# Loading the first Q and K heads as f32 over the hardware queues and casting them on chip, in a fused attention and SwiGLU kernel

## The chip, the cores and the metric

The kernel runs on one core of one Trainium2 chip. The core has a matrix engine (PE, TensorE), a vector engine (DVE), an activation engine (ACT), GpSimd (POOL) and a sync engine (SP). Matrix products read SBUF and write PSUM, which has 8 banks; DVE and ACT read PSUM and write SBUF. DMA transfers between memory and SBUF are issued from POOL (the software queue) or from SP and ACT (the hardware queues), and 16 DMA engines carry them. The metric is the device time of one execution in microseconds (us), as a median of several.

## The reference, cut to what matters

```python
batch, n_heads, seq, head_dim = (8, 12, 448, 64)
scores = scale * np.matmul(q, k.transpose(0, 1, 3, 2))
attn = np.maximum(scores, 0.0) ** 2 / S
x = np.matmul(attn, v)                     # then heads side by side: x is 3584 x 768
rms = np.sqrt(np.mean(x * x, axis=-1, keepdims=True) + 1e-06)
xn = x / rms * rms_g
g = xn @ w_gate                            # 768 x 1536
silu = g * (1.0 / (1.0 + np.exp(-g)))
out = (silu * (xn @ w_val)) @ w_out        # 1536 x 768
```

All inputs and the output are float32. The attention has no softmax: scores go through a relu and a square, so nothing has to be known of a whole row before it is used. The kernel computes in bf16 with f32 accumulation.

## The kernel before, in words

The kernel goes through the 8 batches in order. For each batch it computes the attention of 12 heads, taken as 6 pairs of heads (a pair fills 128 partitions, 64 rows for each head), then a norm over the 768 columns, then the two-layer feed-forward part. The attention of batch b+1 or b+2 is computed while the feed-forward of batch b runs: the weight products come as a "stream" of small steps, and attention work is put between them.

Before the first stream step there is nothing to put the attention between. This stretch is called the head here. In it batch 0 alone is worked on, in two halves of 224 query rows. For a pair of heads the steps are:

- load Q and K: the DMA converts f32 to bf16 on the way. K of batch 0 lands in `wo_sb`, the buffer that later holds the output weights; Q lands in its own tile. (`load`, L278; one load is 2 or 4 heads for batch 0.)
- transposes on PE into a PSUM bank (`transposes`, L412; 14 small products for K at L421 and 8 for Q at L429), then one copy by DVE to `qkT` (L439).
- scores on PE into a pair of PSUM banks (L503, and L521 for the last 64 rows of keys, called the rest), one block of 896 or 448 columns at a time. There are three such pairs of banks in the head.
- relu of the block by ACT (L469) or DVE (L467), then its square by DVE (L472).
- products with V (L607), evicted by ACT (L642), squared by DVE (L646), summed over columns by PE (L904).

When three such sums are in, ACT takes the logarithm and the exponential that make the root of the norm (L712, L716), DVE scales (L721), and the stream of weight products (L856) begins.

The order of instructions on every engine is written out when the kernel is built, by a planner. It keeps a clock for each engine, a cost for each step, and an estimate of when each DMA lands (`arrives` and `pool_dma`: a start after 2.7 us and a rate for each kind of load). It always takes the step that can begin first, and among those that are ready the one of best rank; transposes go before scores. Its times decide only the order; at run time each instruction waits for its own data, but an engine never runs an instruction ahead of one that stands before it.

Where the planner sees PE idle for 0.3 us or more, `fill` (L1118) puts products of ones with zeros there (L1129), as many as fit at 0.1 us each. Their result is not used.

POOL issues all loads on one software queue. A load waits until the eighth load before it has landed. The order for batch 0 is: Q and K of heads 0 and 1, of heads 2 and 3, then the identity matrix for the transposes (made on POOL), Q and K of heads 4 to 7, of heads 8 to 11, then V, then the weights in four slices. SP loads the norm's weights `g_sb` (L380) first; ACT loads a function table first (L392).

Of the kernel before, what the change touches and what calls it, by code (L numbers as in the profile page):

```python
# [8 lines left out]
FP32 = mybir.dt.float32  # L9
BF16 = mybir.dt.bfloat16  # L10
ALU = mybir.AluOpType
ACT = mybir.ActivationFunctionType

NCH = 4
U = 7
# [51 lines left out]
class Planner:  # L67
# [28 lines left out]
    def start(self, op, e, t):  # L96
        for x in op.on:
            self.lists[x].remove(op)
        dur = op.on[e]() if callable(op.on[e]) else op.on[e]
        if e == "PE":  # L100
            dur += self.changed(op.form() if callable(op.form) else op.form)
        self.free[e] = t + dur
        op.engine, op.begun, op.left = e, t, t + dur
        op.done = op.ends(t) if op.ends else t + dur + {"ACT": 0.17, "DVE": 0.13, "PE": 0.22}.get(e, 0.1)
        op.fn(op)
# [67 lines left out]
def kernel(  # L173
# [11 lines left out]
    nc = tc.nc  # L185
    P = nc.NUM_PARTITIONS
    B, H, S, D = q.shape
    T, DM = out.shape
    _, F = moe_w_gate.shape
    assert (T, DM) == (B * S, H * D) and 2 * D == P and S % NCH == 0 and B % 2 == 0 and S == U * D  # L190
    PC = S // NCH
# [34 lines left out]
    def tiles(n, shape, dtype, name):  # L226
        return [work.tile(shape, dtype, name=f"{name}{i}", tag=f"{name}{i}") for i in range(n)]
# [14 lines left out]
    hT = tiles(1, [P, FT, 2 * S], BF16, "hT")[0]  # L242

    plan = Planner(8)
    plan.singles = single
    add = plan.add


    ld, qkT, landed, behind_of = {}, {}, {}, {}
    src_of = {"q": q, "k": k, "v": v}  # L250
    PE_T = 2
    dma_free = [2.2]

    def arrives(kb, rate):
        def ends(t):
            dma_free[0] = max(dma_free[0], t + 2.7) + kb / rate
            return dma_free[0] + 0.2
        return ends

    def pool_dma(cost, kb, rate, start, deps=()):  # L260

        deps = list(deps) + queue[-8:-7]
        queue.append(add(Op({"POOL": cost}, lambda op: start(), deps, ends=arrives(kb, rate))))
        return queue[-1]
# [3 lines left out]
    def stage(nm, b):  # L268
        runs = nm == "v" or b < PE_T
        n, w = (PC, NCH) if nm == "q" else (P, UH)  # L270
        if (nm, b) not in ld:
            shape = [n, H, w * D] if runs else [n, w, H * D]
            ld[nm, b] = ldpool.tile(shape, BF16, name=nm + "b", tag=nm + "b")
            if nm == "k" and runs:
                nc.vector.memset(ld[nm, b][D:, :, (UH - 1) * D :], 0.0)
        return ld[nm, b]

    def load(nm, b, h0=0, h1=H, deps=()):  # L278
        runs = nm == "v" or b < PE_T
        src = src_of[nm][b, h0:h1]  # L280
        if (nm, b) == ("k", 0):

            def runs_of_seven():
                nc.gpsimd.dma_start(
                    out=wo_sb[:D, h0:h1, :S], in_=src.rearrange("h (p u) d -> p h (u d)", p=D)
                )

            ops = [pool_dma(0.7, D * U * D * 4 * (h1 - h0) / 1e3, 300.0, runs_of_seven, deps)]
            landed.setdefault((nm, b), {}).update({h: ops for h in range(h0, h1)})
            return  # L290
        if nm == "q":
            parts = [(slice(0, PC), PC, 0, NCH)]
        else:
            parts = [(slice(0, D), D, 0, UH), (slice(D, P), D, UH if nm == "k" else UH - 1, U)]
        ops = []
        for prt, n, u0, u1 in parts:
            kb = n * (u1 - u0) * D * 4 * (h1 - h0) / 1e3

            def whole(prt=prt, n=n, u0=u0, u1=u1):
                dma = nc.gpsimd.dma_start(  # L300
                    out=stage(nm, b)[prt, h0:h1, : (u1 - u0) * D],
                    in_=src.rearrange("h (p u) d -> p h (u d)", p=n)[:, :, u0 * D : u1 * D],
                )
                if b >= PE_T and not u0:
                    tc.add_manual_dep(dma.ins, turned[b][-1].ins.name, behind)

            if runs:
                ops.append(pool_dma(0.72, kb, (300.0 if nm == 'q' else 345.0) if b == 0 else 400.0, whole, deps))
                continue
            step = u1 - u0 if nm == "q" else 1  # L310
            for u in range(u0, u1, step):

                def piece(prt=prt, n=n, u=u, u0=u0, step=step):
                    to = stage(nm, b)[prt].rearrange("p u (h d) -> p u h d", d=D)
                    rows = src.rearrange("h (p u) d -> p u h d", p=n)
                    behind_of[b] = nc.gpsimd.dma_start(  # L316
                        out=to[:, u - u0 : u - u0 + step, h0:h1, :], in_=rows[:, u : u + step]
                    )

                ops.append(  # L320
                    pool_dma(2.3 if step > 1 else 0.75, kb * step / (u1 - u0), 280.0, piece, deps)
                )
        landed.setdefault((nm, b), {}).update({h: ops for h in range(h0, h1)})

    def new_qkT(b):
        qkT[b] = qtpool.tile([P, HP, 2, S], BF16, name="qkT", tag="qkT")

    turned, made = {}, {}

    def transpose_dma(b, deps):  # L330
        jobs = [("k", c) for c in range(UH)] + [("q", c) for c in range(NCH)]
        turned[b] = []
        for nm, c in jobs:

            def turn(op, nm=nm, c=c):
                if b not in qkT:
                    new_qkT(b)
                n = (P if c < UH - 1 else D) if nm == "k" else PC
                at = c * P if nm == "k" else c * PC
                op.ins = nc.sync.dma_start_transpose(  # L340
                    out=qkT[b][:, :, 0 if nm == "k" else 1, at : at + n], in_=ld[nm, b][:n, c, :]
                ).ins
                if (nm, c) == ("k", 0):
                    tc.add_manual_dep(op.ins, behind_of[b].ins.name, behind)

            need = list(deps) + landed["q", b][0] + landed["k", b][0]
            turned[b].append(add(Op({"SP": 0.1}, turn, need, ends=arrives(170, 120.0))))
# [3 lines left out]
    wo_sb = wpool.tile([P, FT, DM], BF16, name="wo_sb", tag="wo")  # L351
# [21 lines left out]
    busy_bf = const.tile([P, S], BF16, name="busy_bf", tag="busy_bf")  # L373
    nc.vector.memset(busy_bf[:], 0.0)
    ident = const.tile([P, P], BF16, name="ident", tag="ident")
    eps_col = const.tile([P, 1], FP32, name="eps_col", tag="eps_col")
    nc.vector.memset(eps_col[:], eps)
    scrap = const.tile([P, 1], FP32, name="scrap", tag="scrap")
    g_sb = wpool.tile([P, KT], FP32, name="g_sb", tag="rmsg")
    nc.sync.dma_start(out=g_sb[:], in_=moe_rms_g.rearrange("(kt p) -> p kt", p=P))  # L380

    LN_EXP, SILU = 6, 18
    held = [None]
# [4 lines left out]
    def act_set(n):  # L388
        if held[0] != n:
            held[0] = n  # L390
            name = nc.get_next_instruction_name()
            nc.scalar.add_instruction(  # L392
                mybir.InstLoadActFuncSet(name=name, act_func_set_id=n, ins=[], outs=[])
            )

    act_set(LN_EXP)
    plan.free.update({"POOL": 1.3, "PE": 1.3, "DVE": 2.0, "ACT": 2.3, "SP": 1.2})

    behind = mybir.DependencyInfo(mybir.DependencyClass.Sync, mybir.DependencyReason.DATA)

# [342 lines left out]
    class Stream:  # L743
# [8 lines left out]
        def add(self, groups):  # L752
            self.todo += groups
# [364 lines left out]
    def fill(t0, t1):  # L1118
        if not fill_on[0] or t1 - t0 < 0.3:
            return  # L1120
        s = None
        for x in single[::-1]:
            if plan.banks_free(x.banks) <= t0:
                s = x
                break
        if s is None:
            return
        for _ in range(int((t1 - t0 - 0.15) / 0.1)):
            nc.tensor.matmul(out=s.tile[:, :HS], lhsT=ones_bf[:], rhs=busy_bf[:, :HS], start=True, stop=True)  # L1129

    plan.fill = fill

    load("q", 0, 0, 2)
    load("k", 0, 0, 2)
    load("q", 0, 2, 4)
    load("k", 0, 2, 4)
    made["ident"] = add(Op({"POOL": 0.6}, lambda op: masks.make_identity(nc, ident[:])))
    for h in (4, 8):
        load("q", 0, h, h + 4)
        load("k", 0, h, h + 4)  # L1140
    load("v", 0, 0, 6)
    load("v", 0, 6, 12)
    for s in range(NSL):
# [79 lines left out]
```

## Time and profile before

| | us |
|---|---|
| median of 3 runs | 444.3 (443.7 to 445.11) |
| the profiled execution | 441.81 |
| its span, first to last instruction | 440.0 |
| PE busy in the span | 433.7 |
| DVE, ACT, POOL busy in the span | 242.8, 264.5, 77.8 |
| first fill product on PE | 1.30 |
| first transposes on PE | 7.07 |
| first eviction on ACT | 8.92 |
| root of the norm on ACT | 25.59 |
| first weight product on PE | 27.26 |

All times in the trace count from the start of the span. The page shows how long each engine is busy and which groups of instructions cost most; the chain of work follows back from the last instruction, at each step, to what released it. Rows in order of time have the start, the time, the engine, the line, what it writes and reads, and in brackets how long the engine was idle before and what ended that. An engine that is 55% busy over the whole span can still be the one that everything waits for in one stretch of it, so windows of the span are read beside the averages.

### The profile page before, as it was taken

The numbers are of one execution on the slowest core, as the hardware profiler recorded it, in microseconds if no ns is written. First come the engines' busy times: TensorE is split into PE (matmuls) and PEld (weight loads), VectorE is DVE, ScalarE is ACT, GpSimd is POOL, SyncE is SP. The second block draws the span as 40 slices with busy tenths as digits, with TensorE's granted clock in tenths as the row PEclk, the third lists the DMA queues.
The fourth block names the chain that finished last, engine by engine and source line by source line (L and its number), as shares of the span: only waits on it lengthen the run. The fifth ranks groups of instructions, "written<-read, shape, count | busy, mean of one in ns | idle before, by whom it ended". The sixth has DMA issues, their size and how long they took to land.

```text
span 440.0 us, 17134 instructions
## 1 busy us (share of the span) xinstructions
PE 433.7 (99%) x7861; PEld 355.3 (81%) x7861; DVE 242.8 (55%) x414; ACT 264.5 (60%) x389; POOL 77.8 (18%) x98
## 2 busy tenths in 40 slices
PE   8999999999999999999999999999999999999996
PEld 6678877677978997787778997689988998688875
DVE  2977588466746564575655456466755356432210
ACT  3983497677648675675758666576657656342222
POOL 7622620060052053043000340010000000000000
PEclk9999999999999999999999999999999999999999
DMA  8999999799889789799906899781001300020013
GB/s 106 197 204 201 201 192 103 139 175 96 109 89 195 87 143 175 85 146 174 40 4 100 154 183 52 113 145 39 3 4 36 105 9 4 1 85 27 3 37 109
DMA packets 130392, 44.75 MB, mean 102 GB/s; under 512 B 102289, under 2 KB 126865, under 8 KB 130321
## 3 DMA queue, kind: packets, MB, share of 16 engines
q0 software_dynamic: 90944, 24.39, 62.1%
q1 hardware_dynamic: 38992, 18.94, 22.1%
q8 instruction: 61, 1.00, 1.0%
q10 hardware_dynamic: 384, 0.34, 0.3%
q14 instruction: 11, 0.08, 0.1%
HBM read 48.76 MB, written 11.01 MB: 136 GB/s over the span
## 4 chain that ended last, share of the span: by engine, by line
PE 94%; DMA 3%; ACT 2%; issue 0%; DVE 0%; POOL 0%; POOLq 0%
PE psP L856 76%; PE psS L607 7%; PE psS L485 5%; DMA vb<-in_v_dram 3%; PE psP L1129 2%; PE psP L429 1%; PE psS L521 1%; PE psS L503 1%; ACT r L469 1%; ACT acc L469 1%; PE psP L421 0%; ACT x L469 0%; PE psP L904 0%; ACT xT L642 0%; DVE acc L472 0%
## 5 line engine op out<-in xcount | busy, mean ns | idle before, releaser
L856 PE MATMUL psP<-xn,wg_sb 64*64 64x448 bf16 (+1 forms) x2304 | 234.0, 338 | 0.0
L856 PE MATMUL psP<-xn,wv_sb 64*64 64x448 bf16 (+1 forms) x2304 | 216.9, 338 | 1.0 <-issue 1.0
L469 ACT ACTIVATE r<-psS 128x896 bf16<-128x896 f32 (+1 forms) x164 | 145.4, 919 | 61.1 <-PE psS L485 32.9
L856 PEld LDWEIGHTS <-wg_sb 64*64 64x64 bf16 (+1 forms) x2304 | 134.2, 105 | 18.3 <-issue 3.8
L856 PEld LDWEIGHTS <-wv_sb 64*64 64x64 bf16 (+1 forms) x2304 | 134.3, 105 | 14.8 <-issue 3.4
L856 PE MATMUL psP<-wo_sb,hT 64*128 64x384 bf16 (+2 forms) x1563 | 139.8, 321 | 0.0
L472 DVE TENSOR_TENSOR r<-r 128x896 bf16<-128x896 bf16 (+1 forms) x165 | 98.7, 616 | 68.6 <-ACT r L469 67.6
L856 PEld LDWEIGHTS <-hT 64*128 64x128 bf16 (+1 forms) x1563 | 99.8, 97 | 23.9 <-issue 3.5
L941 DVE TENSOR_TENSOR hT<-sil,psP 128x448 bf16<-128x448 bf16 (+1 forms) x108 | 61.0, 566 | 56.7 <-PE psP L856 37.6
L927 ACT ACTIVATE sil<-psP 128x448 bf16<-128x448 f32 (+1 forms) x108 | 54.7, 507 | 57.7 <-PE psP L856 53.9
L1001 ACT COPY ost<-psP 128x384 f32<-128x384 f32 (+1 forms) x52 | 24.5, 471 | 41.0 <-PE psP L856 40.5
L485 PE MATMUL psS<-qkT 64*64 64x448 bf16 (+1 forms) x412 | 48.4, 350 | 0.0
L607 PE MATMUL psS<-r,vb 64*64 64x448 bf16 (+1 forms) x716 | 44.6, 335 | 0.4 <-DMA vb<-in_v_dram 0.2
L300 POOL DMA_DIRECT2D vb<-in_v_dram x20 | 14.3, 725 | 171.5 <-PE psP L856 97.0
L721 DVE SCALAR_TENSOR_TENSOR xn<-xT,g_sb,rstd 128x448 bf16<-128x448 bf16 (+1 forms) x54 | 30.2, 628 | 25.9 <-ACT rstd L716 25.9
L316 POOL DMA_DIRECT2D kb<-in_k_dram x42 | 33.4, 1022 | 19.3 <-DMA vb<-in_v_dram 11.3
L607 PEld LDWEIGHTS <-vb 64*64 64x64 bf16 x756 | 26.6, 106 | 8.6 <-issue 1.6
L642 ACT ACTIVATE xT<-psS 128x896 bf16<-128x896 f32 (+1 forms) x27 | 22.7, 841 | 10.5 <-PE psS L607 10.5
L485 PEld LDWEIGHTS <-qkT 64*64 64x64 bf16 (+1 forms) x412 | 21.7, 103 | 4.1 <-issue 1.1
L392 ACT ACT_TABLE_LOAD x16 | 20.5, 1283 | 1.0 <-PEq L1207 0.7
L652 DVE TENSOR_TENSOR x<-xT 128x896 f32<-128x896 bf16 x14 | 15.2, 1086 | 3.5 <-ACT xT L642 3.5
L654 DVE TENSOR_TENSOR acc<-acc,x 128x896 f32<-128x896 f32 x14 | 15.3, 1092 | 0.5
(58 smaller groups left out, 151.8 us busy)
## 6 DMA issues: line engine op xcount, KB each, us to landing
vb<-in_v_dram POOLq DMA_DIRECT2D x12, 384.0 KB, 8.1
qb<-in_q_dram POOLq DMA_DIRECT2D x6, 672.0 KB, 15.1
kb<-in_k_dram POOLq DMA_DIRECT2D x42, 96.0 KB, 12.4
out_dram<-ost SPq DMA_DIRECT2D x7, 336.0 KB, 3.0
wg_sb<-in_moe_w_gate_dram POOLq DMA_DIRECT2D x4, 576.0 KB, 15.5
wv_sb<-in_moe_w_val_dram POOLq DMA_DIRECT2D x4, 576.0 KB, 17.2
wo_sb<-in_moe_w_out_dram POOLq DMA_DIRECT2D x2, 1152.0 KB, 15.1
out_dram<-ost SPq DMA_DIRECT2D x8, 288.0 KB, 3.0
```

Source lines behind the costliest of these rows:

```text
L316: behind_of[b] = nc.gpsimd.dma_start(out=to[:, u - u0 : u - u0 + step, h0:h1, :], in_=rows[:, u : u + step])
L392: nc.scalar.add_instruction(mybir.InstLoadActFuncSet(name=name, act_func_set_id=n, ins=[], outs=[]))
L469: nc.scalar.activation(out=op.view, in_=src, func=ACT.Relu)
L472: nc.vector.tensor_tensor(out=rl.view, in0=rl.view, in1=rl.view, op=ALU.mult)
L485: nc.tensor.matmul(out=ps[m0:m1, hh, :S], lhsT=qkT[b][prt, j, 0, c * P + m0 : c * P + m1], rhs=qkT[b][prt, j, 1, :], start=True, stop=True,)
L607: mm = nc.tensor.matmul(out=ps[hh * D : (hh + 1) * D, jj, :w], lhsT=vb[prt, 2 * (j + jj) + hh, u * D : (u + 1) * D], rhs=r[prt, hh, :], st ...
L642: nc.scalar.mul(out=xTs[b][:, j : j + 2, lo : lo + w], in_=me.ps.tile[:, :, :w], mul=inv_attn)
L721: nc.vector.scalar_tensor_tensor(out=xns[b][:, kt, lo : lo + w], in0=xTs[b][:, kt, lo : lo + w], scalar=g_sb[:, kt : kt + 1], in1=rstd[:, ...
L856: mm = nc.tensor.matmul(out=self.ps[m0:m1, : self.w], lhsT=self.lhsT(i)[prt, m0:m1], rhs=self.rhs(i)[prt], start=(half == 0 and i == 0), s ...
L927: nc.scalar.activation(out=s[:, :w], in_=g.ps[:, :w], func=ACT.Silu)
L941: nc.vector.tensor_tensor(out=hT[:, fb, o : o + w], in0=sil[b, fb, lo][1][:, :w], in1=g.ps[:, :w], op=ALU.mult,)
L1001: nc.scalar.copy(out=to, in_=g.ps[:, :w])
```

## The change

Heads 0 to 3 of batch 0's Q and K are no longer loaded by POOL with conversion. A new function, `load_exact`, loads them as f32 into `hT` (the buffer for hidden values, not used until the feed-forward part, seen as f32): K from SP's queue, Q from ACT's, two heads in each load. Then DVE or ACT, whichever the planner finds free first, casts them to bf16 into the places where the transposes read them: one step for each head of K, one for two heads of Q. As planned, ACT takes both steps of Q and one of two steps of K in each half, and DVE takes the other step of K.

The loads of heads 4 to 7 become POOL's first, and the identity is made behind them; its zeros are set by DVE. `g_sb` goes behind K on SP, and ACT's table load behind its two issues. The planner's numbers change too: the rate for the loads of batch 0, when the engines are first free, and 0.19 us for a fill product before 5.5 us. As a result 17 fill products stand ahead of the first transposes instead of 42, and the order of the head changes: the transposes of the third and fourth pair come after three score blocks instead of six.

```diff
+    def load_exact(h0, h1):
+        plain = hT.bitcast(FP32)
+        for nm, eng, n, r in (("k", "SP", D, U), ("q", "ACT", PC, NCH)):
+            w = r * D
+            at = slice(h0 + (4 if nm == "q" else 0), h1 + (4 if nm == "q" else 0))
+            def start(op, nm=nm, eng=eng, n=n, at=at, w=w):
+                (nc.sync if eng == "SP" else nc.scalar).dma_start(
+                    out=plain[:n, at, :w],
+                    in_=src_of[nm][0, h0:h1].rearrange("h (p u) d -> p h (u d)", p=n),
+                )
+            moved = add(Op({eng: 0.47}, start, ends=arrives(S * D * 4 * (h1 - h0) / 1e3, 380.0, 1.9), rank=-9))
+            step = 1 if nm == "k" else 2
+            for h in range(h0, h1, step):
+                def cast(op, nm=nm, n=n, h=h, w=w, step=step):
+                    to = wo_sb[:D, h : h + step, :S] if nm == "k" else stage("q", 0)[:, h : h + step, :]
+                    src = plain[:n, h + (4 if nm == "q" else 0) : h + step + (4 if nm == "q" else 0), :w]
+                    if op.engine == "DVE":
+                        nc.vector.tensor_copy(out=to, in_=src)
+                    else:
+                        nc.scalar.copy(out=to, in_=src)
+                c = add(Op({"DVE": 0.07 + step * w * 1.042e-3, "ACT": 0.05 + step * w * 0.833e-3}, cast, [moved], rank=-5))
...
-            ops = [pool_dma(0.7, D * U * D * 4 * (h1 - h0) / 1e3, 300.0, runs_of_seven, deps)]
+            ops = [pool_dma(0.7, D * U * D * 4 * (h1 - h0) / 1e3, 370.0, runs_of_seven, deps)]
...
-                ops.append(pool_dma(0.72, kb, (300.0 if nm == 'q' else 345.0) if b == 0 else 400.0, whole, deps))
+                ops.append(pool_dma(0.72, kb, 370.0 if b == 0 else 400.0, whole, deps))
...
+    nc.vector.memset(ident[:], 0.0)
...
-    nc.sync.dma_start(out=g_sb[:], in_=moe_rms_g.rearrange("(kt p) -> p kt", p=P))
...
-    act_set(LN_EXP)
-    plan.free.update({"POOL": 1.3, "PE": 1.3, "DVE": 2.0, "ACT": 2.3, "SP": 1.2})
+    plan.free.update({"POOL": 1.3, "PE": 1.3, "DVE": 1.4, "ACT": 0.75, "SP": 0.75})
...
-        for _ in range(int((t1 - t0 - 0.15) / 0.1)):
+        while t0 + (0.19 if t0 < 5.5 else 0.1) <= t1 - 0.15:
+            t0 += 0.19 if t0 < 5.5 else 0.1
             nc.tensor.matmul(out=s.tile[:, :HS], lhsT=ones_bf[:], rhs=busy_bf[:, :HS], start=True, stop=True)
...
-    load("q", 0, 0, 2)
-    load("k", 0, 0, 2)
-    load("q", 0, 2, 4)
-    load("k", 0, 2, 4)
-    made["ident"] = add(Op({"POOL": 0.6}, lambda op: masks.make_identity(nc, ident[:])))
-    for h in (4, 8):
-        load("q", 0, h, h + 4)
-        load("k", 0, h, h + 4)
+    load_exact(0, 2)
+    load_exact(2, 4)
+    add(Op({"SP": 0.5}, lambda op: nc.sync.dma_start(out=g_sb[:], in_=moe_rms_g.rearrange("(kt p) -> p kt", p=P))))
+    add(Op({"ACT": 1.3}, lambda op: act_set(LN_EXP), rank=-8))
+    load("q", 0, 4, 8)
+    load("k", 0, 4, 8)
+    made["ident"] = add(Op({"POOL": 0.35}, lambda op: masks.make_identity(nc, ident[:], nomemset=True)))
+    load("q", 0, 8, 12)
+    load("k", 0, 8, 12)
     load("v", 0, 0, 6)
```

More of the change, by code (lines that the diff above doesn't have):

```diff
@@ L252, with arrives @@
     dma_free = [2.2]
-    def arrives(kb, rate):
+    def arrives(kb, rate, begins=2.7):
         def ends(t):
-            dma_free[0] = max(dma_free[0], t + 2.7) + kb / rate
+            dma_free[0] = max(dma_free[0], t + begins) + kb / rate
             return dma_free[0] + 0.2
@@ L323, in load @@
         landed.setdefault((nm, b), {}).update({h: ops for h in range(h0, h1)})
+    def load_exact(h0, h1):
[19 more added lines that the diff above has]
+                c = add(Op({"DVE": 0.07 + step * w * 1.042e-3, "ACT": 0.05 + step * w * 0.833e-3}, cast, [moved], rank=-5))
+                landed.setdefault((nm, 0), {}).update({x: [c] for x in range(h, h + step)})
     def new_qkT(b):
```

## The prediction

> **What bounds the kernel now.** I read the page first, then the chain that ended last over the first 100 us, then the order of time of each engine up to 30 us, and last the DMA by windows.
>
> ```profile
> PE 433.7 (99%) x7861; PEld 355.3 (81%) x7861; DVE 242.8 (55%) x414; ACT 264.5 (60%) x389; POOL 77.8 (18%) x98
> PE psP L856 76%; PE psS L607 7%; PE psS L485 5%; DMA vb<-in_v_dram 3%; PE psP L1129 2%; PE psP L429 1%; PE psS L521 1%; PE psS L503 1%; ACT r L469 1%; ACT acc L469 1%; PE psP L421 0%; ACT x L469 0%; PE psP L904 0%; ACT xT L642 0%; DVE acc L472 0%
> ```
>
> From the first weight product (L856, 27.2 us) to the end TensorE always has work, so what the change can be worth is how much earlier that stage begins. The chain in the head shows what it begins with:
>
> ```profile
> 1.30 5.84 PE psP L1129 x42
> 7.13 0.34 PE psP L421 x14
> ...
> 16.67 2.97 ACT r L469 x4
> ...
> 43.85 0.30 PE psP L1129 x2
> ```
>
> 42 fill products run until 7.06, then the first transposes. Between them and the root of the norm (L712, 25.59 us, the last thing before the stream) ACT and DVE do the evictions, copies and squares:
>
> ```profile
> 8.92 4.05 ACT L469 ACTIVATE r<-psS 128x896 bf16<-128x896 f32 x5 [6.90 <-PE psS L503]
> 13.66 5.98 ACT L469 ACTIVATE r<-psS 128x896 bf16<-128x896 f32 x8 [0.69 <-PE psS L503]
> 25.59 0.45 ACT L712 ACTIVATE rstd<-psP,eps_col 128x224 f32<-128x224 f32 x1 [0.96 <-PE psP L904]
> 10.00:20.00 10.00, 9.90 (x201) 6.25 (x202) 9.91 (x20) 9.25 (x14) 6.58 (x8) 1.00 1.36 194
> 11.36 1.09 DVE L467 TENSOR_SCALAR r<-psS 128x896 bf16<-128x896 f32 x1
> 12.90 1.15 DVE L439 COPY qkT<-psP 128x896 bf16<-128x896 bf16 x2
> 16.93 3.40 DVE L472 TENSOR_TENSOR r<-r 128x896 bf16<-128x896 bf16 x7
> ```
>
> The columns of the window row are PE, PEld, DVE, ACT: from 10 to 20 us DVE is busy 9.91 of 10 us, ACT 9.25. So DVE sets the head, and ACT's 0.69 us gap at 13 us is the wait for the third and fourth pair of heads. Their data is late:
>
> ```profile
> 5.20 0.63 POOL L284 DMA_DIRECT2D wo_sb<-in_k_dram  x1
> 11.94 0.30 PEld L421 LDWEIGHTS <-wo_sb 64*64 64x64 bf16 x14 [0.18 <-DMA wo_sb<-in_k_dram]
> q0 software_dynamic: 549, 0.33, 123.9%
> g_sb<-in_moe_rms_g_dram SPq DMA_DIRECT2D x1, 3.0 KB, 2.2
> ```
>
> K of heads 4 to 7 is issued at 5.20, behind four smaller loads and the identity, and used at 11.94. The third line is the software queue in 7 to 9 us: 165 GB/s written; in 9 to 14 us it is 182.
>
> **The change part by part.** The profiled execution took 441.81 us (span 440.0, 1.8 around it). The median is 444.3, 2.5 above; I sum against 441.81 and move the result by that difference.
>
> *First two pairs of heads.* Two loads each leave at 0.74 and 1.21 from SP and ACT instead of four from POOL at 1.31 to 3.96. They carry 0.92 MB f32. Hardware stores at the end of the span moved 0.34 MB in 28.2% of 16 engines over 4 us, so 302 GB/s at full share; the 3 KB load landed 2.2 us after issue. That gives the first half of the bytes at 0.74 + 1.7 + 1.5 = 4.0, the second at 5.5 to 6.3, the later end if the software queue shares. Casts: ACT's 128x448 evictions (L642) last 0.55, so 0.5 each, two per half on ACT; on DVE one per half, between 0.39 (a square of 448) and 0.55 (half the 1.09 of L467). First transposes at about 5.2 against 7.06. ACT's table load (1.28, L392) now follows its two issues (0.47 each) and ends at 3.0, covered by the wait for 4.0. g_sb goes behind SP's two issues; it is read at 26.5, so free. The identity loses its 0.26 memset to DVE and stands behind two POOL issues (0.73 and 0.63): ready at 3.0 against 4.5. DVE's memset stands ahead of eps_col and holds the first fill by up to 0.1; there is slack of 0.7 at 4.5, where 17 slow fills end. hT holds the f32 until about 6.8 and is first written at 32.1; wo_sb is loaded at 46.5: both waits added are long over.
>
> This start is cover, not gain: the queue reaches the transposes of the third pair at about 8.2 (transposes 0.66 a pair, copies 0.62, three score blocks 0.31 each), against 11.94.
>
> *Heads 4 to 7.* They are now POOL's first loads, issued at 1.31 and 2.1 in place of 4.48 and 5.20. Until K of them is through, 0.92 MB f32 at 302 GB/s (3.0 us) and 0.46 MB of bf16 at 182 (2.5) must go from 2.3 on: 7.9. Landing comes later than that mean: in the trace, the written bytes reached 229 KB, 344 KB and 917 KB at 4.6, 5.5 and 9.6, and the loads landed at 5.2, 6.9 and 11.9: lags of 0.6, 1.4 and 2.3. So 8.5 to 10.2. I take 9.0, since these two now enter an empty queue like the first loads, with lags of 0.6 to 1.4. Heads 8 to 11 follow 2.5 us later (14.46 against 11.9 before), v and the weights as much earlier.
>
> *What follows this landing.* The new order puts the third pair's transposes after three score blocks; the old one after six. So more is left behind them. Counting DVE's instructions from there to the third product of sums: before, 4 copies (0.58), 12 squares of 896 (0.575), 4 of 448 (0.34), 3 of the norm (0.37): 11.7 us. After: two squares of 896 more (1.15), and three 448-wide evictions moved from ACT to DVE (0.54 each, 1.62): 14.5. Of the 2.8 extra, the 0.6 to 0.7 that DVE idled there at 20 to 24 us (0.29, 0.42, 0.19, 0.18) is taken up, so about 2.1 counts. Before, landing to root was 25.59 - 11.94 = 13.65; after it is 15.8. **The head gains 11.94 - 2.1 - 9.0 = 0.8 us**, break-even is a landing at 9.8, and the most is 1.6 (8.2, where the queue arrives).
>
> *The stream.* Before, two fills of 0.30 stand at 43.85, ahead of the last slice of wv; the new order has none. That slice lands about 2 us earlier, with the stream 0.8 earlier: gain 0.3, or 0 if it is late. PE's other fills (86 before the stream, 54 after the change) are idle time already. Behind the head the order differs up to batch 2, with 7 matmuls fewer of 7776; I take 0, with +-0.5 for the one wait there (0.7 on v of batch 2 at 99 us).
>
> Sum: 0.8 + 0.3 = 1.1; 440.7 profiled, **443.2** as a median.
>
> A row and a rule: fills took 0.19 us until about 4.7 and 0.10 after.
>
> ```profile
> 4.00:4.50 0.50, 0.50 (x5) 0.38 (x4) 1.00 1.23 189
> 5.50:6.00 0.50, 0.50 (x8) 0.50 (x6) 1.00 0.83 106
> ```
>
> The Trainium skill, TensorE: Matmul & The Clock Gate, Part 1, says that the array starts at half clock and gets the full one after a busy window of about 3.4 us, in a window that runs freely. That agrees with these two rows. By the rows alone the pace depends on time since the first fill and the sum stays at 1.1; by the rule the pause after 17 fills could spoil two windows, which is an estimate of 11 to 12 us for the full clock and makes the sum the loss of the second rival, priced there from rows.
>
> **Rivals.**
> 1. *The f32 bytes delay the rest (slower).* If written bytes set the pace, 0.92 MB of f32 at 182 GB/s takes 5.0, not 3.0: K of heads 4 to 7 is through at 9.8 and lands at 10.4 to 12.1. The transposes that stand at the head of PE's queue then hold three score blocks whose own data is there. Loss 0.6 to 2.3 less 0.3: 444.6 to 446.3. For it: lags of 2.3. Against: 302 GB/s written by hardware stores. It decides from a landing at 10.1. The Trainium skill, DMA: Bandwidth & Descriptors, Issuing engines are not separate DMA queues, says that transfers issued from different engines interleave on the same 16 and only issue time is saved; no run here yet shows both queues at the head.
> 2. *TensorE stays slow.* 17 fills end at 4.5, PE then waits about 0.7. If the slow pace lasts until 8.4, the two pairs' transposes cost 0.7 more each; the queue reaches the third pair at 9.0, still covered. If until 12, transposes and blocks behind the landing double too, and the root comes 1.3 to 1.9 later than before: 445.3 to 445.9. Against it: one gap only, and PE has the first transposes right after it.
> 3. *Better than summed.* Landing at 8.2 to 8.5 and 0.3 to 0.5 in the stream: gain 1.6 to 2.5, 441.8 to 442.7.
> 4. *Nothing to measure.* Landing at 9.5 to 10: 0 to 0.6 gained.
>
> **How the numbers follow.** Forecast (gain 0.7 to 1.5) 0.40, rival 3 0.24, rival 4 0.18, rival 1 0.11, rival 2 at its long end 0.07. What a measurement of this kernel can tell from no change is about 0.3%, 1.33 us. The forecast lies around that bound: 0.18 of its 0.40 is beyond it. Faster by more: 0.18 + 0.24 = 0.42. Slower by more: of rivals 1 and 2 most, 0.15, and 0.03 for the wait at 99 us. Same: 0.40. Range 441.6 to 445.6; it leaves out the worse halves of rivals 1 and 2 (0.09) and gains above 2.7 (0.07).
>
> **What would show it.** First transposes at 5.0 to 5.6; ACT's first eviction at 7.4 to 8; the third pair's transposes at 8.5 to 9.5 waiting for K; DVE without gaps from 9.7 to 24; root at 24.8; no fill in the stream. A landing after 10, or fills at 0.19 after 8.5, would make it wrong; so would a new wait on weights or v after 27 us.

## The result and the profile after

The changed kernel takes 448.06 us (447.5 to 449.62, six runs) against 443.81 (443.43 to 445.11, six runs) for the kernel before: a ratio of 1.0097, with a 95% interval of 1.0076 to 1.0118. It is 4.25 us slower. The forecast was 443.2, in a range of 441.6 to 445.6.

The profiled execution took 449.62, its span is 447.8. The page shows the first thing to look at: TensorE's busy time and, below the busy tenths, the clock that it was granted.

```profile
PE 436.0 (97%) x7820; PEld 356.0 (79%) x7820; DVE 246.2 (55%) x420; ACT 265.8 (59%) x390; POOL 75.1 (17%) x93
PEclk8599999999999999999999999999999999999999
```

PE has 41 instructions fewer than before and is busy 2.3 us longer. The clock row was all nines before; here its second slice (11 to 22 us) is at 5, half clock. The head in order of time, as the page's groups come when the trace is asked for one stretch:

```profile
1.29 3.33 PE L1158 MATMUL psP<-busy_bf,ones_bf 128*128 128x224 bf16 x17 [1.29 <-DVE busy_bf L402]
5.23 0.39 DVE L346 CAST wo_sb<-hT 64x448 bf16<-64x448 f32 x1 [3.91 <-DMA hT<-in_k_dram]
5.85 0.41 PE L448 MATMUL psP<-ident,wo_sb 64*64 64x64 bf16 x14 [1.22 <-ACT wo_sb L348]
6.50 0.46 PE L1158 MATMUL psP<-busy_bf,ones_bf 128*128 128x224 bf16 x3
9.00 0.39 DVE L346 CAST wo_sb<-hT 64x448 bf16<-64x448 f32 x1 [3.38 <-DMA hT<-in_k_dram]
9.62 0.58 PE L448 MATMUL psP<-ident,wo_sb 64*64 64x64 bf16 x14 [2.65 <-ACT wo_sb L348]
12.48 0.58 PE L448 MATMUL psP<-ident,wo_sb 64*64 64x64 bf16 x14
31.65 0.45 ACT L739 ACTIVATE rstd<-psP,eps_col 128x224 f32<-128x224 f32 x1 [0.97 <-PE psP L931]
```

In the kernel before, the first K transposes stood like this:

```profile
7.07 0.41 PE L421 MATMUL psP<-ident,wo_sb 64*64 64x64 bf16 x14
```

Read the rows of the changed kernel from the top. The 17 fills end at 4.62. K of heads 0 and 1 is cast at 5.23, the first transposes follow at 5.85; that is 1.2 us earlier than before. Then K of heads 2 and 3 is cast only at 9.00, and TensorE waits 2.65 us for it. The second pair's 14 transposes take 0.58 us where the first pair's took 0.41, here as in the kernel before: in this execution TensorE has lost its clock in the wait. The third pair's transposes at 12.48 wait for no data, the queue merely gets there. The root of the norm comes at 31.65, 6.06 later than before.

The chain of waits shows the same from the other end: a DMA now stands at its head, where 42 fills stood before.

```profile
1.56 7.41 DMA hT<-in_k_dram
...
9.00 0.57 ACT wo_sb L348
...
9.62 0.58 PE psP L448 x8
10.20 0.52 PE psP L456 x8
10.71 0.86 PE psS L530 x8
```

The same stretch by windows (PE, PEld, DVE, ACT, POOL, then the granted clock, the DMA share, GB/s):

```profile
8.00:9.00 1.00, 0.00 (x0) 0.00 (x0) 0.00 (x1) 0.00 (x1) 0.00 (x0) 0.54 2.06 166
9.62:21.90 12.28, 12.21 (x182) 7.15 (x182) 8.16 (x15) 6.55 (x8) 7.08 (x9) 0.51 1.37 200
10.00:20.00 10.00, 10.00 (x146) 5.75 (x143) 6.41 (x12) 5.58 (x7) 6.54 (x9) 0.50 1.37 200
20.00:30.00 10.00, 9.09 (x144) 5.44 (x143) 8.04 (x17) 8.29 (x12) 2.25 (x4) 0.91 1.32 204
```

Between 10 and 20 us before, DVE was busy 9.91 and set the head. Now it is busy 6.41, ACT 5.58, and PE 10.00: at half clock TensorE has become the bound of the head. From 0.54 in the window of 8 to 9 us the clock fell at about 8.1, from 0.91 in that of 20 to 30 us it came back at about 21.8.

Part of this is the planner's own filler. It had put eight fill products where it saw TensorE idle; at half clock there is no idle time there, and the chain of waits runs through them:

```profile
11.58 0.48 PE psP L1158 x2
15.91 0.30 PE psP L1158
19.57 1.05 PE psP L1158 x5
```

That is 1.83 us of the chain for products whose result nobody uses. What leaving them out would save was not measured.

And the loads issued in the first 6 us (count, size, median time from issue to landing):

```profile
hT<-in_k_dram SPq DMA_DIRECT2D x2, 224.0 KB, 5.9
hT<-in_q_dram ACTq DMA_DIRECT2D x2, 224.0 KB, 4.2
g_sb<-in_moe_rms_g_dram SPq DMA_DIRECT2D x1, 3.0 KB, 9.7
```

The 3 KB of `g_sb` landed 2.2 us after issue before; the same load now takes 9.7. That more is moved beside it is the likely reason; the runs on `g_sb` and on the software queue below test it.

### The profile page after: what moved, and what is told of

Same layout as the page of the kernel before. It is cut to its first block, busy times and chain, and to the rows that moved or that the text cites. A ratio compares the mean times of both kernels' runs of the same rounds, so it can differ in the third digit from the quotient of the medians.

```text
span 447.8 us, 17060 instructions
## 1 busy us (share of the span) xinstructions
PE 436.0 (97%) x7820; PEld 356.0 (79%) x7820; DVE 246.2 (55%) x420; ACT 265.8 (59%) x390; POOL 75.1 (17%) x93
## 4 chain that ended last, share of the span: by engine, by line
PE 95%; DMA 2%; ACT 1%; issue 1%; DVE 1%; SPq 0%
PE psP L883 76%; PE psS L634 8%; PE psS L512 6%; DMA hT<-in_k_dram 2%; PE psP L456 1%; PE psS L548 1%; PE psS L530 1%; PE psP L1158 1%; PE psP L448 1%; ACT acc L496 1%; ACT r L496 1%; PE psP L931 0%; DVE hT L968 0%; SPq L333 0%; ACT wo_sb L348 0%
## 5 line engine op out<-in xcount | busy, mean ns | idle before, releaser
L883 PE MATMUL psP<-xn,wg_sb 64*64 64x448 bf16 (+1 forms) x2304 | 230.4, 338 | 0.1
L883 PE MATMUL psP<-xn,wv_sb 64*64 64x448 bf16 (+1 forms) x2304 | 212.4, 338 | 1.6 <-issue 1.3
L496 ACT ACTIVATE r<-psS 128x896 bf16<-128x896 f32 x163 | 145.4, 923 | 55.3 <-PE psS L512 31.6
L883 PEld LDWEIGHTS <-wg_sb 64*64 64x64 bf16 (+1 forms) x2304 | 130.7, 105 | 19.0 <-issue 4.5
L883 PEld LDWEIGHTS <-wv_sb 64*64 64x64 bf16 (+1 forms) x2304 | 129.7, 105 | 15.9 <-issue 3.2
L512 PE MATMUL psS<-qkT 64*64 64x448 bf16 (+1 forms) x412 | 49.7, 350 | 0.7 <-issue 0.7
L512 PEld LDWEIGHTS <-qkT 64*64 64x64 bf16 (+1 forms) x412 | 22.6, 103 | 4.9 <-issue 1.8
## 6 DMA issues: line engine op xcount, KB each, us to landing
kb<-in_k_dram POOLq DMA_DIRECT2D x42, 96.0 KB, 12.2
```

The costliest lines, as they stand in the source:

```text
L496: nc.scalar.activation(out=op.view, in_=src, func=ACT.Relu)
L512: nc.tensor.matmul(out=ps[m0:m1, hh, :S], lhsT=qkT[b][prt, j, 0, c * P + m0 : c * P + m1], rhs=qkT[b][prt, j, 1, :], start=True, stop=True,)
L883: mm = nc.tensor.matmul(out=self.ps[m0:m1, : self.w], lhsT=self.lhsT(i)[prt, m0:m1], rhs=self.rhs(i)[prt], start=(half == 0 and i == 0), s ...
```

## The experiments

Three theories on the loss were set up. A: `g_sb`'s load, 3 KB in 768 small pieces right behind K on SP, holds up K of heads 2 and 3. B: the loads on the software queue, now issued from 1.3 us on, take the DMA engines from the f32 loads. C: whatever made that K late, the price is TensorE's clock, lost in the wait. `more` in the edits below is the number of extra fill products in the first pause (4.6 to 5.85) and in the second (before the second pair's transposes). A and B are about the cause of the lateness and can both hold; C is about what it costs. Rows of order of time below are the K transposes of a pair (14 products on PE) and the root (ACT), unless something else is said. K's 14 transposes are also the clock's gauge: 0.41 us at full pace, 0.58 at half.

### Giving TensorE work in the two pauses (theory C)

```diff
+    more = [7, 24]
...
+        n = more.pop(0) if more else 0
         while t0 + (0.19 if t0 < 5.5 else 0.1) <= t1 - 0.15:
             t0 += 0.19 if t0 < 5.5 else 0.1
+            n += 1
+        for _ in range(n):
             nc.tensor.matmul(...)
```

The loads, the casts and the order of everything else stay; 31 more fill products whose result is not used are the only difference.

> The changed kernel with 7 more fill products before the first transposes and 24 more between the first and the second pair's transposes, where TensorE stood idle for 1.2 and 2.65 us; all else in the same order. Theory C (the pause costs the full clock from 8.3 to 22 us, and that half clock is the larger part of the loss): the clock stays full after about 5, the root of the norm comes at 27.5 to 28.5 instead of 31.65, and the loss falls from 4.2 to 0.5 to 1.5 us. Theories A and B alone: the clock does not matter, the loss stays at 3.5 to 5.

Measured: 443.89 us (443.04 to 444.81, ten runs), a ratio of 0.9989 to the kernel before (0.9975 to 1.0002).

```profile
9.05 0.41 PE L448 MATMUL psP<-ident,wo_sb 64*64 64x64 bf16 x14 [0.16 <-ACT wo_sb L348]
10.79 0.41 PE L448 MATMUL psP<-ident,wo_sb 64*64 64x64 bf16 x14
26.57 0.45 ACT L739 ACTIVATE rstd<-psP,eps_col 128x224 f32<-128x224 f32 x1 [0.96 <-PE psP L931]
```

And its window of 10 to 20 us:

```profile
10.00:20.00 10.00, 9.45 (x187) 5.62 (x183) 9.38 (x19) 9.21 (x13) 6.19 (x8) 1.00 1.37 201
```

All transposes are at full pace, DVE is busy 9.38 of 10 us again, and the root is 5.08 us earlier than in the changed kernel. The whole measured loss is gone, more than the 0.5 to 1.5 us that were expected to remain. K of heads 2 and 3 is still late (transposes at 9.05), so with the pauses filled its lateness costs no time that can be measured here. C holds: the price is the half clock.

Two runs split the pauses, with `more = [7, 0]` and `more = [0, 24]`.

> The changed kernel with 7 more fill products ahead of the first transposes only (24 instead of 17), everything else in its order. It has two pauses of TensorE early on: 1.2 us between the fills and the first transposes (4.6 to 5.85) and about 2.7 us between the first and the second pair's transposes (6.9 to 9.6). Theory C1, the first pause costs the clock: the full clock stays from 5 us on, root near 27, time 443.5 to 444.8. Theory C2, the second pause costs it: full clock from about 4.9 to 8.5, half until about 22, root near 31.5, time 447.3 to 449. Rival D, any one pause is enough: as C2.

> The changed kernel with 24 more fill products ahead of the second pair's transposes only; the 17 ahead of the first transposes stay, and so does the pause of 1.2 us at 4.6. C2 (the second pause costs the clock): full clock from 4.9 on or at the latest from 8.4, root 26.5 to 27.5, time 443.5 to 445. C1 or D (the first pause is enough): half clock until after 15 us, time 447 to 449.

Only the first pause filled: 448.35 (448.05 to 449.29), ratio 1.0099 (1.0071 to 1.0127). The second pair's transposes and the root:

```profile
9.65 0.58 PE L448 MATMUL psP<-ident,wo_sb 64*64 64x64 bf16 x14 [2.77 <-ACT wo_sb L348]
31.93 0.45 ACT L739 ACTIVATE rstd<-psP,eps_col 128x224 f32<-128x224 f32 x1 [0.96 <-PE psP L931]
```

Only the second pause filled: 444.71 (444.13 to 446.04), ratio 1.002 (1.0 to 1.0041).

```profile
5.79 0.58 PE L448 MATMUL psP<-ident,wo_sb 64*64 64x64 bf16 x14 [1.16 <-ACT wo_sb L348]
10.63 0.41 PE L448 MATMUL psP<-ident,wo_sb 64*64 64x64 bf16 x14
12.37 0.41 PE L448 MATMUL psP<-ident,wo_sb 64*64 64x64 bf16 x14
28.15 0.45 ACT L739 ACTIVATE rstd<-psP,eps_col 128x224 f32<-128x224 f32 x1 [0.96 <-PE psP L931]
```

The second pause, the one between the two pairs, costs the clock. Here TensorE was still at half pace at 5.79 and the 27 fills ran long (until 10.6), so the root is 1.6 later than with both pauses filled and later than the 26.5 to 27.5 expected.

The clock need not be lost in that pause; it may not have come by then. In a second profile of the changed kernel (run again unchanged, see below) the first pair's transposes are already at half pace, the second pair's are too, after a pause of 1.71, and the root is at 31.48 all the same:

```profile
5.68 0.58 PE L448 MATMUL psP<-ident,wo_sb 64*64 64x64 bf16 x14 [1.05 <-ACT wo_sb L348]
```

Either way it is the unfilled pauses that leave the head at half pace.

### The other half of the change alone: fewer fills

```diff
-        for _ in range(int((t1 - t0 - 0.15) / 0.1)):
+        for _ in range(17 if t0 < 2.0 else int((t1 - t0 - 0.15) / 0.1)):
```

This is the kernel before with 17 fills instead of 42 ahead of the first transposes; a second run has 24.

> The kernel before with 17 fill products ahead of the first transposes instead of 42, and nothing else changed. First transposes at 5.6 to 5.8 instead of 7.1 in any case. Theory C: the pause after the fills delays or costs the full clock, 1 to 3 us slower. Theories A and B: nothing that waits for it moves, since the third pair's K lands at 11.9 as before; within 0.5 us of the kernel before.

> The kernel before with 24 fill products in the first stretch instead of 42; nothing else. The first transposes go from 7.07 to 5.4, with no pause of TensorE, so the full clock comes at about 5.0 as before. If the wait for K of heads 4 to 7 (11.9) sets the head, nothing is gained: 443.3 to 444.5. If the first evictions count as well (ACT and DVE begin 1.6 us earlier, and the 0.6 to 0.7 us of idle time of DVE behind the landing stays), the gain is 0.5 to 1.5: 442.5 to 443.5. A loss would say that the fills are needed for more than the clock.

With 17: 442.05 (441.47 to 447.35, five runs), ratio 0.9963 (0.9926 to 1.0001). With 24: 444.67 (441.25 to 446.17, twelve runs), ratio 0.9997 (0.9971 to 1.0022). First, second and third pair and the root, with 17 fills:

```profile
5.38 0.58 PE L421 MATMUL psP<-ident,wo_sb 64*64 64x64 bf16 x14 [0.76 <-DMA wo_sb<-in_k_dram]
8.32 0.58 PE L421 MATMUL psP<-ident,wo_sb 64*64 64x64 bf16 x14
12.22 0.41 PE L421 MATMUL psP<-ident,wo_sb 64*64 64x64 bf16 x14
25.87 0.45 ACT L712 ACTIVATE rstd<-psP,eps_col 128x224 f32<-128x224 f32 x1 [0.96 <-PE psP L904]
```

and the third pair and the root with 24:

```profile
11.72 0.41 PE L421 MATMUL psP<-ident,wo_sb 64*64 64x64 bf16 x14 [1.04 <-DMA wo_sb<-in_k_dram]
25.37 0.45 ACT L712 ACTIVATE rstd<-psP,eps_col 128x224 f32<-128x224 f32 x1 [0.97 <-PE psP L904]
```

Fewer fills alone lose nothing in the median, where theory C had been taken to mean 1 to 3 us for the 17, and starting the first pair 1.4 to 1.7 us earlier gains nothing that can be told: the third pair stands at 11.7 to 12.2, as before, when its K is there. They are not free of risk: three of the twelve executions with 24 fills have a mean granted clock of 0.987 to 0.992 and took 446.0 to 446.2, and one of the five with 17 has 0.987; none of 23 of the kernel before is under 0.996. With 17 fills the profile has TensorE at half pace until the second pair and at the full one again at 12.2. Other work and fills follow there without a long wait; that this is why the clock comes back is likely and not tested. So fewer fills lose little by themselves, and a late K with the wait filled loses nothing: it is the late K with the wait left open that costs the clock.

### Why K of heads 2 and 3 is late

Theory A, first with `g_sb` moved off the start: its load waits for the copy of the last pair of heads. Then the opposite, `g_sb` ahead of K on SP as in the kernel before.

```diff
-    add(Op({"SP": 0.5}, lambda op: nc.sync.dma_start(out=g_sb[:], ...)))
+    def load_g(op):
+        dma = nc.sync.dma_start(out=g_sb[:], ...)
+        tc.add_manual_dep(dma.ins, turned[0][5].ins.name, behind)
+    add(Op({"SP": 0.5}, load_g, [Turned(0, 5)]))
```

```diff
     g_sb = wpool.tile([P, KT], FP32, name="g_sb", tag="rmsg")
+    nc.sync.dma_start(out=g_sb[:], in_=moe_rms_g.rearrange("(kt p) -> p kt", p=P))
...
-    add(Op({"SP": 0.5}, lambda op: nc.sync.dma_start(out=g_sb[:], ...)))
```

> The changed kernel, but g_sb's load (768 pieces of 4 bytes, on SP behind the two K loads) waits for the copy of the last pair of heads, some 17 us. Theory A (the K load of heads 2 and 3 lands at 9.0 instead of 6 because g_sb's small packets stand behind it on the same queue and share the engines): K of heads 2 and 3 lands at 6 to 7, the second pair's transposes move from 9.6 to 7 to 7.5, TensorE's pause before them falls from 2.65 to under 1 us, and the loss of 4.2 us falls to 0 to 2. Theory B (the software queue's loads take the engines): the landing stays at 8.5 or later and the loss at 3.5 to 5. Theory C (the half clock alone): landing and loss as in A only if the clock also stays full after 8.3.

> The changed kernel, but g_sb's load stands first on SP, ahead of K, as it did before. Theory A: its packets find empty engines (9 ns each before, 20 to 160 ns now), so K of heads 0 and 1 comes 0.5 to 0.8 later than 5.2, but heads 2 and 3 land at 7 to 7.5 instead of 9.0; loss 1 to 3 us. Theory B: K of heads 2 and 3 lands at 9 to 10, loss 4 to 5.5.

Later: 448.33 (447.09 to 448.41), ratio 1.0086 (1.006 to 1.0111). First: 450.35 (449.29 to 451.24), ratio 1.0137 (1.0109 to 1.0164). The cast of K of heads 2 and 3 with `g_sb` later, then the casts of K of heads 0 and 1 and of heads 2 and 3 with `g_sb` first:

```profile
8.14 0.39 DVE L346 CAST wo_sb<-hT 64x448 bf16<-64x448 f32 x1 [2.83 <-DMA hT<-in_k_dram]
```

```profile
7.54 0.39 DVE L346 CAST wo_sb<-hT 64x448 bf16<-64x448 f32 x1 [6.22 <-DMA hT<-in_k_dram]
10.19 0.39 DVE L346 CAST wo_sb<-hT 64x448 bf16<-64x448 f32 x1 [2.26 <-DMA hT<-in_k_dram]
```

`g_sb` ahead of K costs 2.3 us of landing for heads 0 and 1 (7.54 against 5.23; 0.5 to 0.8 had been expected) and 1.2 for heads 2 and 3 (10.19 against 9.00), and the median is 2.3 us above that of the changed kernel. Behind K it seemed at first to cost 0.9 (9.00 against 8.14), but that did not hold: in the five profiles with `g_sb` right behind K and the loads unchanged this cast stands at 8.43, 8.54, 8.95, 9.00 and 9.04, in the three with it later at 8.14, 8.89 and 8.94. The two overlap. So small pieces ahead of a load on its queue do delay it, in this one profile, but A, which has them behind it, is not shown.

Theory B: POOL's first load waits for the cast of Q of heads 0 and 1, so that the software queue moves nothing in the first 5 us. The identity is made ahead of the loads, and 13 more fills bridge the pauses; the order of all engines but POOL is unchanged.

```diff
+        held_back = len(queue) < 8
+        if held_back:
+            deps += landed["q", 0][0]
-        queue.append(add(Op({"POOL": cost}, ..., ends=arrives(kb, rate))))
+        queue.append(add(Op({"POOL": cost}, ..., ends=arrives(kb, rate, -10.0 if held_back else 2.7))))
...
+                if nm == "q" and b == 0 and h0 == 4:
+                    tc.add_manual_dep(dma.ins, landed["q", 0][0][0].ins.name, behind)
...
+    more = [7, 6]
```

> The changed kernel with POOL's first load waiting for the cast of Q of heads 0 and 1 (about 4.7 us), so that the software queue moves nothing while the f32 loads are under way; the identity is made ahead of the loads, and fills bridge the two pauses of TensorE (7 and 6 more). Theory B, the software queue's loads take the engines from the second pair's K: its casts begin at 6.0 to 7.0 instead of 9.0, the second pair's transposes at 7 to 7.6; heads 4 to 7 then land later, at 11 to 12 instead of 10.2, and the root comes at 26.5 to 28: time 443.5 to 445.5. Rival E, the second load on SP is slow by itself (its own descriptors or the order on SP): casts still at 8 to 9, with heads 4 to 7 later as well: 445 to 447.

Measured: 446.13 (444.11 to 448.46, ten runs), ratio 1.0043 (1.0021 to 1.0066). The second pair's cast, POOL's K load of heads 4 to 7, the transposes of the second, third and fifth pair, and the root:

```profile
6.06 0.63 POOL L287 DMA_DIRECT2D wo_sb<-in_k_dram  x1
7.09 0.52 DVE L351 CAST wo_sb<-hT 64x448 bf16<-64x448 f32 x1 [1.55 <-DMA hT<-in_k_dram]
7.75 0.41 PE L453 MATMUL psP<-ident,wo_sb 64*64 64x64 bf16 x14
10.89 0.41 PE L453 MATMUL psP<-ident,wo_sb 64*64 64x64 bf16 x14 [1.32 <-DMA wo_sb<-in_k_dram]
15.35 0.58 PE L453 MATMUL psP<-ident,wo_sb 64*64 64x64 bf16 x14 [2.06 <-DMA wo_sb<-in_k_dram]
30.65 0.45 ACT L744 ACTIVATE rstd<-psP,eps_col 128x224 f32<-128x224 f32 x1 [0.96 <-PE psP L936]
```

With the software queue silent, K of heads 2 and 3 is cast at 7.09 instead of 8.4 to 9.0: in this one profile sharing the DMA engines is worth 1.3 to 1.9 us of its lateness, B holds for that much. The rest against the forecast of 5.5 to 6.3 stands without any sharing with POOL. The second thing to see is the load of heads 4 to 7. It was issued at 6.06 instead of 2.12 and was there when the transposes began, at 10.89. In the changed kernel it landed 7.8 us after its issue, at 9.92: 3.9 us of later issue cost about 1 us of landing. So at the start the bytes set the landing far more than the issue. The third is half clock in another place: heads 8 to 11 now come late, TensorE waits 2.06 us, and the transposes behind that wait are at 0.58. So B's half of the expectation held and the rest missed: root at 30.65 for 26.5 to 28, time 446.13 for 443.5 to 445.5. Whether this wait took the clock is not shown: by the granted clock it fell only 0.1 us into it, as worked out below.

### Looking for a version that beats both

The first run has both repairs, `g_sb` later and `more = [7, 18]`. The second adds 260 GB/s instead of 370 in the planner's estimates for batch 0, which puts two more score blocks ahead of the third pair's transposes.

```diff
-            ops = [pool_dma(0.7, D * U * D * 4 * (h1 - h0) / 1e3, 370.0, runs_of_seven, deps)]
+            ops = [pool_dma(0.7, D * U * D * 4 * (h1 - h0) / 1e3, 260.0, runs_of_seven, deps)]
...
-                ops.append(pool_dma(0.72, kb, 370.0 if b == 0 else 400.0, whole, deps))
+                ops.append(pool_dma(0.72, kb, (260.0 if nm == 'q' else 260.0) if b == 0 else 400.0, whole, deps))
```

> The changed kernel with both repairs: g_sb's load waits for the copy of the last pair of heads (worth 0.9 us of the second pair's landing), and 7 and 18 more fill products bridge TensorE's two pauses so that the clock stays. If the clock was the loss and the late second pair most of the rest, the second pair's transposes stand at 8.7, the third's at 10.3 to 10.6, and the root at 26.1 to 26.4, 15.8 behind them as in the run with fills alone (26.57 - 10.79): time 443.0 to 443.8, within 0.3% of the kernel before. If g_sb's place takes something back elsewhere: 444 or more.

> As the one with both repairs, but the planner is told 260 GB/s instead of 370 for batch 0's loads, so that two more score blocks stand ahead of the third pair's transposes, as in the kernel before. If DVE's backlog behind these transposes costs the 2.1 us that the prediction gave it, the transposes stand at 11 to 11.6 and the root 13.7 behind them, at 24.7 to 25.4, earlier than in the kernel before (25.6): time 442.3 to 443.3. If the backlog only moves ahead of the transposes, the root stays at 26 to 26.5: 443 to 444.

Both repairs: 445.58 (444.34 to 449.62, twelve runs), ratio 1.0037 (1.0005 to 1.007). With the other order as well: 444.91 (443.42 to 446.54, twelve runs), ratio 1.0007 (0.9983 to 1.0031). Neither beats the kernel before. Third pair and root of the one, then of the other:

```profile
11.26 0.41 PE L448 MATMUL psP<-ident,wo_sb 64*64 64x64 bf16 x14
27.03 0.45 ACT L739 ACTIVATE rstd<-psP,eps_col 128x224 f32<-128x224 f32 x1 [0.96 <-PE psP L931]
```

```profile
12.50 0.39 PE L448 MATMUL psP<-ident,wo_sb 64*64 64x64 bf16 x14
26.25 0.45 ACT L739 ACTIVATE rstd<-psP,eps_col 128x224 f32<-128x224 f32 x1
```

The first expectation failed in its start: `g_sb`'s place gave nothing, K of heads 2 and 3 came at 8.89, and with 18 fills in place of 24 three of the twelve runs (447.66, 449.45, 449.62) have a mean granted clock of 0.988 or 0.989 where the other nine have 0.998 or more. The clock seems to be kept with no margin there. The second run came out by the second branch of its expectation: the root stands 13.75 behind the third pair's transposes instead of 15.77, but they come 1.24 later, at 12.50 and not at 11 to 11.6. Most of DVE's backlog only moved ahead of them, the root is at 26.25, the head gains 0.8 and not 2, and the time is above both ranges (442.3 to 444).

### Both kernels once more

> The kernel before, unchanged, for a second profile: its first one took 441.81, less than any of 29 later executions but none behind it in the head, so the question is what a usual execution has more. If the head varies: a root other than 25.6 by a microsecond or two. If TensorE's stalls on its own instruction stream vary: root at 25.3 to 25.9, and 1 to 6 us of such stalls in the stream.

> The changed kernel, unchanged, for a second profile: its first one took 449.62, 1.6 above its median. If the head varies: second pair's casts not at 9.0, root off 31.65 by a microsecond or more. If the stream varies: root at 31.3 to 32, transposes of the second pair at half pace (0.58 for K's 14) again, and the span 446 with fewer stalls.

They took 442.79 and 449.45. The heads end as in the first profiles: roots at 25.38 (25.59) and 31.48 (31.65). What TensorE waits for in the stream, from 40 us on, is one line, of before:

```profile
PE psP L856 <- issue: 2.7, 4, 1.2
```

That is 2.7 us in four waits that no other engine and no data explains; in the first profile of before it was 1.0, and in that with 17 fills 6.0. Counting all of TensorE's waits from 40 us on, the four profiles in the order of before have 1.2, 2.6, 2.7 and 6.0 us (mean 3.1), the nine in the new order 0 to 2.5 (mean 1.4).

## Why the prediction was wrong, point by point

In short: the step that failed is the landing of the second pair's bytes, summed at 5.5 to 6.3 and measured at 9.0, and with it the wait of TensorE for them, which the sum put at nothing. What that wait cost was not its length but the half clock behind it: 4.5 of the 6.85 us by which the root was late against the forecast.

*First two pairs of heads.* The first half of the step held for Q, cast at 4.14 (forecast 4.0), and less well for K, cast at 5.23 where 4.0 was summed for both; the first transposes stood at 5.85 (5.0 to 5.6). The second half failed. Its bytes were to be there at 5.5 to 6.3, "the later end if the software queue shares"; K of heads 2 and 3 was cast at 9.00, and at 7.09 even without sharing. This is the step that broke. The rate of 302 GB/s came from stores at the end of the span that had the engines to themselves. In the changed kernel all queues together moved 189 GB/s from 5 to 9 us; with POOL held back the two hardware queues alone moved 262 from 2 to 3.5 us and 223 from 3.5 to 5 (in the changed kernel, with the software queue beside them, all together 262 and 205). None of these comes to 302. SP's second load also left later than summed, at 1.56 and not at 1.21.

*"This start is cover, not gain".* The start was indeed no gain: the kernel before with 24 fills shows it. But it was not free cover. A second pair 3 us late made a hole in TensorE's queue, and that hole had a price of its own. The queue reached the third pair's transposes at 12.48 instead of 8.2; with the clock kept, at 10.79.

*TensorE stays slow (the second rival).* This is what happened, and it had 0.07. Its mechanism, fills ending too soon and a pause behind them, was the right one. What was wrong was which pause, and the price. The rival looked at the gap of 0.7 us at 4.5; filling that one alone changed nothing. The gap of 2.65 us before the second pair was not seen, because its load had been given 5.5 to 6.3. And "until 12" was the long end, with 1.3 to 1.9 us of loss; the clock was at half until 21.8. The second sentence against it, PE has the first transposes right after it, was no protection: they last 1.1 us, with the three fills behind them.

*Heads 4 to 7.* Taken at 9.0, bounds 8.5 to 10.2. It landed 7.8 us after its issue at 2.12, at 9.92, towards the late end. By the prediction's own sum this alone would have left no gain (11.94 - 2.1 - 9.92 = -0.1). It did not decide, since the queue was later still. The first rival's idea, bytes and not issue times set the landing, is supported by the run that held POOL back; its price cannot be told apart from the rest.

*What follows this landing.* The size of this term was right to a few hundredths. In all four profiles of before's order the root stands 13.65 behind the third pair's transposes, in those of the new order at full clock 15.78, 15.77 and 15.78 (10.79 to 26.57, 11.26 to 27.03, 12.37 to 28.15); the forecast was 15.8, with 2.1 of extra DVE work that counts. That the longer backlog costs this much is shown by the run with the third pair's transposes two blocks later (13.75). That it fits to a few hundredths is partly luck, since two parts were off and cancel. From the third pair's transposes to the third product of sums DVE's busy time grew by 2.2 (12.12 before, 14.33 with both pauses filled), not by 2.8; and its idle time there, taken as 0.6 to 0.7 though the rows listed for it add up to 1.08, hardly shrank (1.08 to 1.00).

*The sum of the head.* The root was to come at 24.8, and came at 31.65, 6.85 later. From the third pair's transposes to the root 19.17 instead of 15.78 makes 3.39, from the second pair's to the third's 2.86 instead of 1.74 makes 1.12: together 4.5 for the clock. The other 2.36 is the late second pair: 9.62 and 1.74 make 11.36, where 9.0 was summed.

*The stream.* The 0.3 cannot be read: the two orders put different work between the products. The root is 6.06 later, but the medians differ by 4.25 only, and with both pauses filled the root is 1.0 later and the time no longer. One would think that the new order gets something back behind the root, but the profiles do not show it: from the root to the end of the span the four in the order of before take 414.4 to 419.7 us, the nine in the new order 413.6 to 417.1, and in the two first profiles the changed kernel takes 1.7 more. The waits counted above (mean 3.1 against 1.4) scatter from profile to profile in the same way. Why TensorE waits there, and whether the order matters for it, stays open.

*How long the half clock lasts.* The windows give the length of the half-clock stretches. In the changed kernel it is 8.1 to 21.8, so 13.7. In the run that held POOL back two windows serve:

```profile
13.30:15.30 2.00, 0.00 (x0) 0.00 (x0) 1.23 (x3) 1.03 (x2) 0.82 (x1) 0.53 1.37 184
15.35:22.00 6.65, 6.43 (x101) 3.96 (x101) 4.02 (x8) 2.98 (x5) 4.10 (x5) 0.63 1.35 201
```

0.53 puts the fall at 13.4, 0.63 the return at 20.3, so 6.9. TensorE's last products before the wait end at 13.3, so the clock fell 0.1 us into it. The Trainium skill, TensorE: Matmul & The Clock Gate, Part 1, tells of a free-running window of 3413 ns; four and two of these make 13.7 and 6.8, so on the length of the steps the trace agrees. By the table there the full clock is back after one busy window and lost after an idle one. Here the first does not agree by the profile's busy time, in which the ends of products are modelled: TensorE was busy 12.21 of the 12.28 us from 9.62 to 21.90 and the clock stayed at half. The second is open: in the 3.41 us ahead of the fall TensorE was busy for 1.12 in the changed kernel, but for 2.40 with POOL held back, which is no idle window. What decides it, no run here shows.

## What to carry to other kernels

Products that only keep TensorE busy are part of the schedule: when a load in front of them moves, put the filler where the wait now is, not where it used to be, and reckon that a wait of about 2 us in a head can cost the half clock for many microseconds behind it, not only its own length. Filler placed on idle time at full clock stands in the way at half clock. Before giving the first loads a rate, look for a row in which as many queues move as much at once; a load that gets the engines to itself is no measure for the start. And where a landing is set by bytes, issuing earlier or over another queue mostly changes who is late.

## What the runs showed of the hardware that was not expected

- TensorE's clock did not come back while it was busy with the head's small products: 12.21 of 12.28 us busy by the profile, 64x64 transposes and 64-row score products mostly, all at half clock. With 17 fills in the kernel before it was there at 12.2 us, after half pace up to the second pair.
- Behind waits of 2.06, 2.65 and 2.77 us the transposes took 0.58, behind waits of 1.04 to 1.32 us on a TensorE at full pace 0.41. The length of the wait is not the whole rule: the granted clock fell 0.1, 1.1 and 2.0 us into the three long ones (in the last, the run with only the first pause filled, it is still 0.99 over 6.90 to 8.90, in a wait that began at 6.88).
- The clock row can't be trusted for the first part of a span. In the second profile of the changed kernel it reads 1.00 between 10 and 20 us, and in that with `g_sb` first it is all nines, while K's transposes take 0.58 there. Fills of 0.19 us stand under a 1.00 as well. The durations of one kind of product are the safer gauge.
- A load of 3 KB in single words of 4 bytes landed 2.2 us after its issue with next to nothing beside it, 5.1 mostly beside the f32 loads alone, and 9.7 beside these and the software queue.
